# Weight tiles of 256 rows by 256 columns in a one-core attention and two-MoE kernel, with a new program order

## The chip, the cores and the metric

The kernel runs on one core of a Trainium2 chip. Its engines are TensorE (PE, with its weight loads as PEld), VectorE (DVE), ScalarE (ACT), GpSimd (POOL) and SyncE (SP), which issues nearly all DMAs. The metric is the device time of one execution in microseconds (us). Before the change it is 809.87 us, the median of three runs (809.11 to 810.15).

## The reference

Windowed attention with 32 global tokens per head, then a max-MoE of three matrices, then a gated MoE. All arrays are float32 in the reference; the weights reach the device as float64, as pairs of 32-bit words.

```
# q_l, k_l, v_l: (4, 8, 512, 64); q_g, k_g, v_g: (4, 8, 32, 64); window 32
out_g = softmax(q_g @ [k_g, k_l]^T / 8) @ [v_g, v_l]
out_l = softmax([q_l @ k_g^T / 8, masked(q_l @ k_l^T / 8)]) @ [v_g, v_l]
x = concat(out_g, out_l) as (2176, 512)
h = max(max(x @ w1, x @ w2), x @ w3)        # w1, w2, w3: (512, 768)
x = h @ w_out                               # w_out: (768, 512)
out = (sigmoid(x @ w_gate) * (x @ w_val)) @ w_out2
```

## The kernel before

**Stages.** From 0 to about 400 us attention and the first MoE run interleaved; from there to the end the second MoE runs, with dense matmuls. Tokens come in eight chunks `c` (four batches, two halves of 256 tokens each, the second with the 32 global tokens). A unit `t` is a pair of heads of a chunk. For the first two chunks PE transposes q and k (`tq`, `tk`, L532), DVE and ACT copy them out (`qw` L553, `kw` L557), PE makes scores (`sp`, L619), DVE masks them and takes the row minimum (`sm`, L625), ACT takes the exponential (L661), DVE multiplies by the reciprocal sum (`sm`, L675), PE transposes the result (`tp`, L683), ACT and DVE copy the two halves out (`pw`, L686 and L688), and PE multiplies with v (`ot`, L770). The result is scaled by ACT (`xw`, L790) and is the input of the first MoE.

**Weights of the first MoE.** `conv_a(i)` loads one raw tile of 512 KB (L302 for w1, w2, w3; L305 for `w_out`), 24 in all, 18 of them of the first three matrices. Tile `(wi, f)` holds all 512 rows (4 blocks of 128, `KD` = 4) of 128 columns, so a row of it is 1 KB in DRAM. Four steps turn float64 words into float32 (L287 on DVE or L285 on ACT, L289 on ACT, L291 and L294 on DVE), then ACT rounds a high part (L312) and POOL subtracts to get the low part (L271). The tile is then `ww[wi, f]` (whole float32) and `wa[wi, f]` (high and low).

**Layer 1.** `moe1_l1(c, f, wi, hold)` makes 128 output columns `f` of matrix `wi` for chunk `c`: four accumulating matmuls into a PSUM tile `ps` for chunk 0 (L882, whole float32), twelve for the other chunks (L321 to L323, three products of high and low parts). ACT copies the first of the three matrices out (`h`, L890), DVE takes the maximum with the second and third (L896, L893). The PSUM pool of `ps` has three buffers, which `tq` and `tk` share. Layer 2 (`moe1_l2`, L918 and L321 to L323) needs all six `f`.

**Order.** Every step is an entry of the list `ev`. The table `ORDER`, 3388 numbers, fixes in which order the entries are emitted, and with it the order of every engine and of the DMA queue; each engine runs its instructions strictly in that order. `SLOT` gives each raw and converted tile its place in SBUF.

Of the kernel before, what the change touches and what calls it, by code (L numbers as in the profile page):

```python
# [17 lines left out]
P = 128  # L18
# [185 lines left out]
def kernel(  # L204
# [92 lines left out]
    def conv_a(i):  # L297
# [8 lines left out]
        yield  # L306
        yield from to_f32(raw, i in LOW_ACT_A)
        hi = f32(raw[:, :, 1])
        ww[wi, f] = hi.rearrange("p (k f) -> p k f", k=KD) if cols else hi
        yield  # L310
        t = slot(("w", i), (2, DM), F32R)
        nc.scalar.copy(t[:, 0], hi)  # L312
# [1164 lines left out]
```

## Time and profile before

| what | us |
|---|---|
| median of three runs | 809.87 |
| the profiled execution, its own time | 809.25 |
| span of the profiled execution, first to last instruction | 807.5 |
| PE busy in it | 789.1 |
| DVE busy | 605.0 |
| ACT busy | 466.8 |
| POOL busy | 146.2 |

The profile is of one execution; 1.75 us of its time lie outside its span. PE is the busiest engine, so what counts is where PE is idle, and which engine or transfer ends each of these waits. Times in rows are us from the start of the span.

### The profile page before, as it was taken

Reading aid. Unit: us, or ns where it says so; the run is one execution under the profiler, and the core shown is the slowest. Engines: PE = TensorE matmul, PEld = TensorE weight load, DVE = VectorE, ACT = ScalarE, POOL = GpSimd, SP = SyncE. Lnnn points to the kernel's source line nnn. Section 1 sums busy time; section 2 is a strip of 40 time slices with the busy share of each in tenths; the row PEclk is TensorE's granted clock in tenths of the full one; section 3 lists DMA queues with packets and bytes.
Section 4 is the critical chain, followed back from the end, with each engine's and each line's share of the span. In section 5 each row is a group of like instructions: output and inputs, shape, how many; then the busy total and the mean of one; then the engine's idle time right before and its main releaser. Section 6 shows DMA issues by size and latency. Waiting matters only on the chain.

```text
span 807.5 us, 18056 instructions
## 1 busy us (share of the span) xinstructions
PE 789.1 (98%) x6854; PEld 751.9 (93%) x6854; DVE 605.0 (75%) x1303; ACT 466.8 (58%) x1119; POOL 146.2 (18%) x149
## 2 busy tenths in 40 slices
PE   6899999999999999999999999999999999999998
PEld 4678899999999899999999999999999999999998
DVE  4999987857766686863876878877675869876963
ACT  6887665747455584562657666665545366544532
POOL 3232566343242423332120000000000000000000
PEclk9999999999999999999999999999999999999999
DMA  9986545545456466454335266757252379635311
GB/s 211 265 232 171 120 93 101 112 82 118 88 104 116 95 106 104 77 99 114 140 101 184 92 185 210 242 194 235 99 179 82 121 253 314 196 109 187 118 43 56
DMA packets 217591, 116.08 MB, mean 144 GB/s; under 512 B 161056, under 2 KB 204576, under 8 KB 217504
## 3 DMA queue, kind: packets, MB, share of 16 engines
q1 hardware_dynamic: 216960, 114.80, 53.4%
q8 instruction: 54, 0.88, 0.5%
q14 instruction: 33, 0.27, 0.1%
q10 hardware_dynamic: 544, 0.13, 0.1%
HBM read 74.91 MB, written 28.57 MB: 128 GB/s over the span
## 4 chain that ended last, share of the span: by engine, by line
PE 86%; DVE 4%; ACT 3%; DMA 2%; SPq 2%; issue 1%; POOL 1%; DVEq 0%; POOLq 0%; ACTq 0%
PE pa L1038 18%; PE ps L321 9%; PE pe L1038 9%; PE ps L323 9%; PE ps L322 9%; PE pa L1225 9%; PE pb L1038 4%; PE pe L1225 4%; PE ps L882 3%; PE sp L619 3%; PE pb L1225 2%; PE ot L780 2%; PE ps L918 1%; PE acc L1202 1%; DMA pt<-pc 1%
## 5 line engine op out<-in xcount | busy, mean ns | idle before, releaser
L1038 PE MATMUL pa<-m,m 128*128 128x384 f32 (+1 forms) x864 | 155.0, 326 | 0.0
L321 PE MATMUL ps<-xt,m 128*128 128x288 f32 (+1 forms) x504 | 148.0, 294 | 1.7 <-DVE h L896 1.3
L323 PE MATMUL ps<-xt,m 128*128 128x288 f32 (+1 forms) x504 | 146.8, 291 | 0.0
L322 PE MATMUL ps<-xt,m 128*128 128x288 f32 (+1 forms) x504 | 145.1, 288 | 0.0
L1038 PEld LDWEIGHTS pa<-m,m 128*128 128x128 f32 x864 | 144.5, 188 | 0.1
L1044 ACT COPY sn<-pa 128x384 f32<-128x384 f32 (+1 forms) x108 | 49.5, 462 | 90.3 <-PE pa L1038 85.7
L321 PEld LDWEIGHTS ps<-xt,m 128*128 128x128 f32 x504 | 94.7, 188 | 6.9 <-issue 2.6
L322 PEld LDWEIGHTS ps<-xt,m 128*128 128x128 f32 x504 | 94.7, 188 | 0.1
L323 PEld LDWEIGHTS ps<-xt,m 128*128 128x128 f32 x504 | 94.6, 188 | 0.0
L1038 PE MATMUL pe<-m,m 128*128 128x384 f32 (+1 forms) x432 | 82.1, 327 | 0.0
L1038 PEld LDWEIGHTS pe<-m,m 128*128 128x128 f32 x432 | 72.6, 188 | 0.2 <-DVE sgt L1057 0.2
L1225 PE MATMUL pa<-m,m 128*128 128x256 f32 x576 | 72.2, 283 | 0.0
L1225 PEld LDWEIGHTS pa<-m,m 128*128 128x128 f32 x576 | 70.5, 192 | 0.1
L896 DVE TENSOR_TENSOR h<-ps,h 128x288 f32<-128x288 f32 (+1 forms) x90 | 39.1, 436 | 38.8 <-PE ps L323 30.0
L661 ACT ACTIVATE sm<-sm,st 128x224 f32<-128x224 f32 x128 | 60.9, 480 | 12.2 <-DVE st L625 12.1
L271 POOL TENSOR_TENSOR h<-h,h 128x288 fp32r<-128x288 f32 (+1 forms) x42 | 39.0, 932 | 105.3 <-ACT h L901 95.0
L707 DVE TENSOR_TENSOR pc<-sm,pc 64x512 f16<-64x512 f32 (+1 forms) x72 | 54.1, 751 | 3.6 <-ACT pc L704 1.7
L625 DVE CUSTOM_DVE_ANT_0 sm<-sp,mask 128x224 f32<-128x224 f32 x128 | 45.4, 381 | 6.7 <-PE sp L619 6.1
L1163 ACT CAST m<-m 128x768 fp32r<-128x768 f32 x44 | 35.8, 836 | 24.5 <-PE pa L1225 7.5
L1168 DVE TENSOR_TENSOR m<-m,m 128x768 fp32r<-128x768 f32 x44 | 41.1, 955 | 11.6 <-ACT m L1163 10.7
L321 PE MATMUL ps<-h,m 128*128 128x288 f32 (+1 forms) x168 | 49.2, 293 | 0.0
L322 PE MATMUL ps<-h,m 128*128 128x288 f32 (+1 forms) x168 | 48.6, 289 | 0.6 <-POOL h L271 0.6
(194 smaller groups left out, 1624.2 us busy)
## 6 DMA issues: line engine op xcount, KB each, us to landing
m<-in_moe_w_dram SPq DMA_DIRECT2D x18, 512.0 KB, 5.1
gd<-sgt SPq DMA_DIRECT2D x48, 192.0 KB, 3.6
m<-gd SPq DMA_DIRECT2D x6, 1536.0 KB, 7.8
m<-in_moe_w_val_dram SPq DMA_DIRECT2D x6, 1024.0 KB, 5.4
wr<-in_moe_w_out_dram SPq DMA_DIRECT2D x6, 1024.0 KB, 6.2
m<-in_moe_w_gate_dram SPq DMA_DIRECT2D x5, 1024.0 KB, 5.6
vr<-in_v_l_dram SPq DMA_DIRECT2D x48, 96.0 KB, 2.6
x2d<-x2s SPq DMA_DIRECT2D x32, 128.0 KB, 2.0
```

Of the source, the lines that this page charges most:

```text
L271: nc.gpsimd.tensor_tensor(out=out, in0=a, in1=f32(b), op=ALU.subtract)
L321: nc.tensor.matmul(ps, lhsT=wh, rhs=xh, start=first, stop=False)
L322: nc.tensor.matmul(ps, lhsT=wh, rhs=xl, start=False, stop=False)
L323: nc.tensor.matmul(ps, lhsT=wl, rhs=xh, start=False, stop=last)
L625: nc.vector.tensor_tensor_reduce(out=sm[:, hh, j], in0=sp[hh][:, j, 0:224], in1=mask[:, half + j, :], scale=-SC, scalar=3.0e38, op0=ALU.ad ...
L661: nc.scalar.activation(sm4[:, i], sm4[:, i], AF.Exp, bias=st[:, 0, i:i + 1], scale=-1.0, accum_out=st[:, 2, i:i + 1])
L707: nc.vector.tensor_tensor(out=l_, in0=s_, in1=h_, op=ALU.subtract)
L896: nc.vector.tensor_tensor(out=a, in0=ps[:, 0:n], in1=a, op=ALU.max)
L1038: nc.tensor.matmul(ps, lhsT=w[l][:, a, i], rhs=x[m][:, i], start=(k in (1, 2, 5) and i + l + m == 0), stop=(k in (2, 3, 4) and i == 1 and ...
L1044: nc.scalar.copy(t[:, 0:n], pend[u]["a"][:, 0:n])
L1168: tt(out=lo, in0=src[op], in1=f32(hi), op=ALU.subtract)
L1225: nc.tensor.matmul(ps, lhsT=g[l][:, f], rhs=wo_op(b, f, m), start=(k in (1, 2, 5) and f + l + m == 0), stop=(k in (2, 3, 4) and f == 5 and ...
```

## The change

`conv_a` loads, for w1, w2 and w3, tiles of 256 rows by 256 columns instead of 512 rows by 128 columns: tile `(wi, f)` is now column pair `f // 2` and row half `f % 2`. It is 512 KB as before, but a row of it is 2 KB in DRAM. `moe1_l1` takes its four row blocks from two tiles, `(wi, f - f % 2)` for the first two and the next one for the last two, and picks its 128 columns in them. `w_out`, the conversion steps, the number and size of matmuls and the `SLOT` table stay as they are. `ORDER` is another permutation of the same 3388 entries.

```
 ORDER = [
-    0, 57, 56, 62, 63, 64, 67, 68, 69, 256, 58, 74, 70, 75, 76, 59, 71, 153, 154, 77, 155, 78, 87, 1854, 161, 162, 79,
...
     def conv_a(i):
         f, wi = divmod(i, 3) if i < 3 * NF1 else (i - 3 * NF1, 3)
+        fp, kh = divmod(f, 2)
         src, cols = (w1, w2, w3, w_out)[wi], wi < 3
         raw = slot(("raw", i), (DM, 2), I32)
         if cols:
-            nc.sync.dma_start(out=raw.rearrange("p (k f) t -> p k (f t)", k=KD),
-                              in_=src[:, f * 2 * P:(f + 1) * 2 * P].rearrange("(k p) f -> p k f", p=P))
+            nc.sync.dma_start(out=raw.rearrange("p (k f) t -> p k (f t)", k=2),
+                              in_=src[kh * 2 * P:(kh + 1) * 2 * P, fp * 4 * P:(fp + 1) * 4 * P].rearrange("(k p) f -> p k f", p=P))
...
-        ww[wi, f] = hi.rearrange("p (k f) -> p k f", k=KD) if cols else hi
+        ww[wi, f] = hi.rearrange("p (k f) -> p k f", k=2) if cols else hi
...
-        wa[wi, f] = t.rearrange("p l (k f) -> p l k f", k=KD) if cols else t
+        wa[wi, f] = t.rearrange("p l (k f) -> p l k f", k=2) if cols else t
...
         ps = ps_mm.tile([P, CH], F32, tag="mm", name="ps1")
+        cols = slice(P * (f % 2), P * (f % 2) + P)
+        tiles = [(wi, f - f % 2 + k // 2) for k in range(KD)]
         if c in WHOLE1:
             for k in range(KD):
-                nc.tensor.matmul(ps[:, 0:n], lhsT=ww[wi, f][:, k], rhs=xt[c, k][:, 0, 0:n], start=(k == 0), stop=(k == KD - 1))
+                nc.tensor.matmul(ps[:, 0:n], lhsT=ww[tiles[k]][:, k % 2, cols], rhs=xt[c, k][:, 0, 0:n], start=(k == 0), stop=(k == KD - 1))
         for k in range(KD) if c not in WHOLE1 else ():
-            wt = wa[wi, f]
+            wt = wa[tiles[k]]
             x = xt[c, k]
-            mm3(ps[:, 0:n], (wt[:, 0, k], wt[:, 1, k]), (x[:, 0, 0:n], x[:, 1, 0:n]), k == 0, k == KD - 1)
+            mm3(ps[:, 0:n], (wt[:, 0, k % 2, cols], wt[:, 1, k % 2, cols]), (x[:, 0, 0:n], x[:, 1, 0:n]), k == 0, k == KD - 1)
```

Three places of the new order are shown. Line numbers of the changed kernel are one higher than before up to `moe1_l1`, and three higher in it and behind it. The first is the head of SP's DMA queue: `m_134` and `m_96` are q, `m_138` and `m_89` the last k rows with the global k, `m_137` and `m_88` the other k rows of chunk 0, each before and now.

```order
L432 DMA m_134<-in_q_l_dram 128x2x64 x2
L442 DMA m_138<-in_k_l_dram 32x8x64
L443 DMA m_138<-in_k_g_dram 32x8x64
L440 DMA m_137<-in_k_l_dram 128x6x64 x2
L432 DMA m_134<-in_q_l_dram 128x6x64 x2
L302 DMA m_180<-in_moe_w_dram 128x4x256
L385 DMA qgr<-in_q_g_dram 32x4x32 x4
```

```order
L443 DMA m_89<-in_k_l_dram 32x8x64
L444 DMA m_89<-in_k_g_dram 32x8x64
L433 DMA m_96<-in_q_l_dram 128x2x64 x2
L433 DMA m_96<-in_q_l_dram 128x6x64 x2
L441 DMA m_88<-in_k_l_dram 128x6x64 x2
L303 DMA m_186<-in_moe_w_dram 128x2x512
L303 DMA m_196<-in_moe_w_dram 128x2x512
L386 DMA qgr<-in_q_g_dram 32x4x32 x4
```

The last k rows now go ahead of the first q, and a weight tile has 512 words in a row instead of 256. The second place is PE around the first groups of layer 1, chunk 0.

```order
L683 MATMUL tp<-ident,sm 128x128 x8
L770 MATMUL ot<-pw,m_404 64x128 x16
L645 MATMUL sg<-kw,qgz_82 64x256 x2
L647 MATMUL sg<-kw,qgz_82 64x32 x2
L619 MATMUL sp<-kw,qw 128x224 x4
L645 MATMUL sg<-kw,qgz_82 64x256 x2
L882 MATMUL ps_568<-xw,m_376 128x256 x4
L882 MATMUL ps_581<-xw,m_235 128x256 x4
L882 MATMUL ps_588<-xw,m_180 128x256 x4
L683 MATMUL tp<-ident,sm 128x128 x8
```

```order
L684 MATMUL tp<-ident,sm 128x128 x8
L620 MATMUL sp<-kw,qw 128x224 x4
L646 MATMUL sg<-kw,qgz_82 64x256 x2
L648 MATMUL sg<-kw,qgz_82 64x32 x2
L646 MATMUL sg<-kw,qgz_82 64x256 x2
L771 MATMUL ot<-pw,m_425 64x128 x16
L885 MATMUL ps_569<-xw,m_241 128x256 x2
L885 MATMUL ps_569<-xw,m_374 128x256 x2
L684 MATMUL tp<-ident,sm 128x128 x4
L885 MATMUL ps_585<-xw,m_359 128x256 x2
L885 MATMUL ps_585<-xw,m_196 128x256 x2
```

The scores `sp` and `sg` moved from behind the products `ot` to ahead of them, and a group of layer 1 now reads two weight tiles. The third place is DVE a little earlier, between two multiplications L675 (L676 now).

```order
L667 RECIPROCAL st_238<-st_238 128x4
L675 TENSOR_TENSOR sm_237<-sm_237,st_238 128x896
L688 COPY pw_380<-tp_343 128x512
L287 TENSOR_SCALAR m12_376<-m12_376 128x512
L667 RECIPROCAL st_350<-st_350 128x4
L675 TENSOR_TENSOR sm_349<-sm_349,st_350 128x896
```

```order
L668 RECIPROCAL st_228<-st_228 128x4
L689 COPY pw_367<-tp_361 128x512
L676 TENSOR_TENSOR sm_227<-sm_227,st_228 128x896
L287 TENSOR_SCALAR m12_359<-m12_359 128x512
L287 TENSOR_SCALAR m14_374<-m14_374 128x512
L668 RECIPROCAL st_372<-st_372 128x4
L676 TENSOR_TENSOR sm_371<-sm_371,st_372 128x896
```

The copy `pw` of one half of the transposed scores now stands ahead of the multiplication for the next pair of heads.

## Rows read from the trace of the kernel before

**Rows 1.** The page: busy us, share of the span, instructions of the engines
```profile
PE 789.1 (98%) x6854; PEld 751.9 (93%) x6854; DVE 605.0 (75%) x1303; ACT 466.8 (58%) x1119; POOL 146.2 (18%) x149
```
**Rows 2.** Busy time by stretch: length, busy us per engine, clock, DMA share, GB/s
```profile
0.00:15.60 15.60, 9.70 (x38) 6.26 (x39) 5.59 (x23) 7.64 (x27) 6.36 (x26) 1.00 0.91 217
15.60:38.00 22.40, 17.60 (x164) 12.58 (x162) 21.88 (x56) 20.19 (x67) 4.44 (x4) 1.00 0.97 259
38.00:60.00 22.00, 20.19 (x108) 17.02 (x107) 20.39 (x55) 17.14 (x45) 8.65 (x6) 1.00 0.86 222
60.00:100.00 40.00, 39.80 (x277) 32.99 (x275) 39.79 (x93) 29.19 (x79) 14.57 (x11) 1.00 0.60 149
100.00:400.00 300.00, 297.61 (x3535) 280.79 (x3535) 215.94 (x607) 175.61 (x519) 108.05 (x99) 1.00 0.52 101
400.00:800.00 400.00, 400.00 (x2711) 398.26 (x2710) 299.37 (x472) 215.98 (x386) 4.15 (x4) 1.00 0.50 163
800.00:807.50 7.50, 4.22 (x36) 4.02 (x34) 2.08 (x4) 1.07 (x2) 0.00 (x0) 1.00 0.22 72
```
**Rows 3.** PE's waits: releaser, us in total, times, longest us
```profile
PE tq L532 <- DMA m<-in_q_l_dram: 4.5, 3, 3.1
PE tp L683 <- DVE sm L675: 1.8, 2, 1.4
...
PE tq L532 <- ACT h L890: 1.3, 1, 1.3
PE ps L321 <- DVE h L896: 1.3, 2, 1.0
...
PE ps L882 <- ACT kw L557: 0.5, 1, 0.5
```
**Rows 4.** PE's timeline: start, us, instruction, [idle before, releaser]
```profile
4.33 0.64 PE L532 MATMUL tk<-ident,m 128*128 128x128 f32 x2
5.42 0.34 PE L532 MATMUL tk<-ident,m 64*128 64x64 f32 x1 [0.46 <-DMA m<-in_k_g_dram]
...
19.90 0.33 PE L532 MATMUL tq<-ident,m 128*128 128x128 f32 x1 [0.87 <-DMA m<-in_q_l_dram]
...
27.06 1.09 PE L683 MATMUL tp<-ident,sm 128*128 128x128 f32 x8 [1.44 <-DVE sm L675]
...
34.00 1.86 PE L770 MATMUL ot<-pw,m 96*64 96x128 f32 x29 [1.13 <-DVE pw L688]
...
36.43 1.03 PE L619 MATMUL sp<-kw,qw 64*128 64x224 f32 x8
37.38 0.65 PE L645 MATMUL sg<-kw,qgz 128*64 128x256 f32 x4
37.97 5.46 PE L882 MATMUL ps<-xw,m 128*128 128x256 f32 x24
```
**Rows 5.** DMA totals of 24.95 to 27.85 (nearly all 1 KB packets)
```profile
DMA packets 1050, 1.05 MB, mean 362 GB/s; under 512 B 32, under 2 KB 1049, under 8 KB 1049
```
**Rows 6.** The same of 430 to 431.95 (nearly all 2 KB packets, of w_gate)
```profile
DMA packets 388, 0.79 MB, mean 403 GB/s; under 512 B 6, under 2 KB 6, under 8 KB 388
```
**Rows 7.** DVE's timeline between 16 and 34 us (columns as in rows 4)
```profile
16.78 0.42 DVE L287 TENSOR_SCALAR m<-m 128x512 int32<-128x512 uint32 x1
17.21 0.39 DVE L625 CUSTOM_DVE_ANT_0 sm<-sp,mask 128x224 f32<-128x224 f32 x1
...
17.84 0.69 DVE L294 SCALAR_TENSOR_TENSOR m<-m 128x512 int32<-128x512 int32 x1
...
22.75 1.47 DVE L294 SCALAR_TENSOR_TENSOR m<-m 128x512 int32<-128x512 int32 x1
...
28.06 1.09 DVE L675 TENSOR_TENSOR sm<-sm,st 128x896 f32<-128x896 f32 x1
...
33.25 0.70 DVE L688 COPY pw<-tp 128x512 f32<-128x512 f32 x1
```
**Rows 8.** POOL's timeline between 20 and 25 us
```profile
22.20 1.47 POOL L271 TENSOR_TENSOR m<-m,m 128x512 fp32r<-128x512 f32 x1 [14.62 <-ACT m L312]
```

337 rows, old and new, of the table ORDER are left out of this document.

## The prediction

> **What bounds the kernel now.** I read the page's totals first: PE is busy 789.1 us of a span of 807.5 [rows 1]. The change keeps every matmul, so only the remaining 18.4 us in which PE is idle can be won, plus whatever new waits it makes. Next, busy time by stretch [rows 2]: subtract PE's busy time from each length. PE idles 5.9 us up to 15.6, 4.8 from there to 38, 1.8 from 38 to 60, 0.2 from 60 to 100, 2.4 from 100 to 400, nothing from 400 to 800 and 3.3 in the last 7.5. The granted clock is 1.00, the upper level of 2.4 GHz, in every stretch, so no term below is a clock term. The DMA column is 0.91 and 0.97 in the first two stretches: loading is a limit there and nowhere else. DVE is busy 21.88 of 22.40 us in the second stretch and 39.79 of 40.00 from 60 to 100: there DVE is as full as PE. The list of PE's waits [rows 3] then says who ends them: q transfers (4.5 us in three waits, 3.1 of them the unavoidable first), DVE's multiply L675 (1.8), ACT's copy `h` (1.3) and DVE's maximum L896 (1.3 in two waits, behind 60). The question is which of some 12 us of waits before 60 go, and whether the time so won lasts until 400, where DVE-bound stretches can take it back.
>
> **The change part by part.**
>
> *Larger rows in DRAM.* Eighteen loads of 512 KB change from 1 KB rows to 2 KB rows. In 24.95 to 27.85, with nearly only 1 KB packets, the queue moved 362 GB/s [rows 5]; in 430 to 431.95, with nearly only 2 KB packets, 403 GB/s [rows 6]. 524288 bytes take 1.45 us at the first rate and 1.30 at the second: 0.15 us saved per tile. Where the queue is full, everything behind a tile lands that much earlier. Three tiles stand in the queue ahead of the q transfer that ends the wait of 0.87 at 19.90 [rows 4]: 3 x 0.15 = 0.45 us. PE's work up to that point is the same in both orders, so I take −0.45 there. The bounds are 0, if the transpose is then held by its input's successors instead (the copy `qw` comes next), and −0.87, the whole wait.
>
> The Trainium skill (DMA: Bandwidth & Descriptors, section "Where 436 GB/s comes from") says that loads from HBM into SBUF are bound on the HBM side, at about 358 GB/s. By it a tile would take an estimated 1.46 us in either shape and this term would be nothing. The trace shows 403 GB/s in a load of 2 KB rows [rows 6], above that figure, so here the measurement decides. That rule's outcome is a rival below.
>
> *Head of the queue.* The six first transfers are the same bytes in another order: the last k rows first, then q, then the rest of k. The sixth still lands at about 5.3 us. Before, what was left for PE at that time was one transpose of 64 columns, 0.34 us at 5.42; now the transposes that wait for the last of them take 0.64 us, as the two at 4.33 do [rows 4]. The first scores may begin some 0.3 to 0.6 us later. This ends in the wait for q at 19.90 (0.87 us, a DMA's), of which 0.42 are left after the term above, so it is absorbed: 0 taken, 0.6 − 0.42 = +0.2 as a bound.
>
> *From 19.90 to the first group of layer 1* (PE's row 96 in both orders, at 37.97 before [rows 4]). Two waits lie here that the order touches. At 34.00 PE waited 1.13 us for DVE's copy `pw` before the products `ot`. In the new order the scores `sp` and `sg` stand ahead of them, work that lies between 35.86, the end of the products, and 37.97 before: 2.1 us of cover for a wait of 1.13. It goes, unless `pw` is more than a microsecond later. At 27.06 PE waited 1.44 us for the multiply L675. In DVE's order the copy `pw` now goes ahead of the multiply. That gives the products their operand earlier by one multiply (1.09 us at 28.06) and makes the next transpose wait for a copy of 0.70 more [rows 7], but PE has work of that stretch to put in between. DVE itself is full, so I count its work up to the copy that stood at 33.25: one L287 fewer (−0.42), one L625 (+0.39) and one step L291 more (+0.69, as its twin L294 at 17.84): +0.66 us. Against this one two-input step fewer coincides with POOL: at 22.20 POOL's subtraction ran 1.47 us, and DVE's L294 at 22.75 took 1.47 instead of 0.69 [rows 7, 8], so one collision costs 0.78. The two cancel within 0.12. What is left is the 1.13 us wait, and of the 1.44 one the net of the swap, 1.09 − 0.70 = 0.39: −1.52 taken. The bounds are −2.57, both waits whole, and 0, if `pw` slips by as much as it was moved. Layer 1 then starts at 37.97 − 0.45 − 1.52 = 36.0.
>
> *A copy `xw` behind the last product.* The products now end right at the first group. Its third and fourth matmuls need the last two `xw`. A group is four matmuls in 1.82 us (5.46 for three groups [rows 4]), so two of them cover 0.9 us, and a copy of 128 x 256 can be bounded by the 0.70 us that one twice its size took on DVE [rows 7]. Nothing taken; +0.5 if ACT is late.
>
> *From 38 to 60.* Layer 1 of chunk 0 now takes two tiles per group but gets two groups from them, so its first three groups need six tiles instead of three. In DVE's order the last step of the sixth tile stands seven instructions behind the last copy `pw`, some 5 us of work; the third group begins 36.0 + 2 x 1.82 + 1.0 (transposes `tp`) = 40.6, and by that count the tile is ready at 39 to 40. The transpose `tq` then waited 1.3 us for a PSUM buffer, held by ACT's `h`, which stood behind the conversions [rows 3]. Now eight transposes `tp` stand between the three groups, so `tq` comes 1 us later relative to the first group while `h` can leave from the end of the first: the wait goes. The 0.5 us wait of layer 1 for `kw` [rows 3] goes in the same way. Against these 1.8 us I set 0.8 for a new wait of the groups for converted tiles, as DVE is at 20.39 of 22.00 us there [rows 2]. Taken: −1.0; bounds −1.8 and +1.0.
>
> *From 60 to 400.* PE arrives 3.0 us earlier (0.45 + 1.52 + 1.0) where DVE was full for 40 us [rows 2]. Its work there is the same, so what PE gained beyond DVE's own lead is given back in waits for L625, L675 or L896. DVE's lead is the conversion work that PE no longer waits for; I give back 0.9 us, the size of one of the waits for L896 (1.3 us in two, the longest 1.0 [rows 3]). Bounds: 0 and +5, which is seven chunks with about 0.7 each.
>
> *From 400 on.* PE has no idle time up to 800 [rows 2], the matmuls and the tail are the same: 0.
>
> **The sum.** −0.45 − 1.52 − 1.0 + 0.9 = −2.07 us. The profiled execution took 809.25 us (span 807.5, and 1.75 outside it, which stays), so this becomes 807.18. The median of the runs, 809.87, is 0.62 above the profiled one; with the same offset the forecast is 807.8.
>
> **The rivals.**
>
> *Six tiles instead of three (no change).* If DVE is later by the three extra conversions, the third group waits for them. A tile costs DVE an L291 and an L294, 2 x 0.69 = 1.4 us, and one more L287 of 0.42 where ACT doesn't do it [rows 7]. One and a half such tiles, 2.1 to 2.7 us, eat the gain between 20 and 60: with all of 1.52 + 1.0 = 2.5 us gone and 0.9 no longer there to give back, 809.87 − 0.45 = 809.4. For it speaks that DVE is busy 98% in 15.6 to 38 [rows 2]; against it that the counts up to the copy `pw` differ by under 0.1 us.
>
> *The PSUM pool in 100 to 400 (slower).* Layer 1 in later chunks uses three buffers `ps`, freed by `h` on ACT and by L896 on DVE. The new order interleaves other work there, and a wait for L896 cost up to 1.0 us, 1.3 in two [rows 3]. Without what is given back behind 60, the forecast would be 807.8 − 0.9 = 806.9. If each of the seven later chunks meets one more wait of 0.7 us on the average, the time is 806.9 + 4.9 = 811.8. It turns to slower, 811.5, from 4.6 us of such waits: five more than now at 1.0 each. Against it: DVE is busy 215.94 of 300 us there [rows 2], so it has room to catch up.
>
> *The shape brings nothing.* If the queue is bound elsewhere, as by the rule quoted above, the 0.45 us fall away: 808.25, the rest standing. For it speaks that the second stretch moved a mean of 259 GB/s at a DMA share of 0.97 [rows 2], so much of that time is not large packets.
>
> **How the numbers follow.** A change of 0.2% (1.6 us) is about what a measurement of this kernel can tell from none: below 808.25 is faster, above 811.5 slower. Chances: the forecast 0.56, six tiles 0.22, the PSUM pool 0.14, no gain from shape 0.08. The forecast lies only 0.45 us inside the bound of faster: so of its 0.56 some 0.08 are for times that land above it, within 0.2%, and 0.48 for faster; the last rival stands on the bound, 0.04 each way; the six-tile rival is within it, 0.22; the PSUM rival is slower, 0.14. Faster 0.52, same 0.34, slower 0.14. The range: the lower end takes the gain of 38 to 60 at its bound (0.8 more), nothing given back (0.9), the whole wait at 19.90 (0.42 more) and the rest of the 1.44 us wait (1.05): 807.8 − 3.2 = 804.6. The upper end takes in the six-tile rival and the pool rival up to 0.6 us per chunk (806.9 + 4.2 = 811.1), half of its chance: 811.1.
>
> **What would show it right or wrong.** Right: PE's first matmul of L885 (L882 before) starts near 36 us; the wait for q near 19.5 is under 0.5; no wait of `ot` for `pw` and none of `tq` for `h` in 38 to 60; a window with only weight tiles moves about 400 GB/s. Wrong: `ps` waits for DVE's L294 near 40 us (six tiles); a list of waits in 100 to 400 with five or more for the maximum, 4 us together (PSUM pool); still 362 GB/s in tile loads (shape). If PE is idle over 0.2 us anywhere from 400 to 800, the term of 0 there is wrong.

## The result and the profile after

The changed kernel takes 816.12 us, the median of six runs (814.46 to 819.62), against 810.01 for the kernel before; the ratio is 1.0082 (95% interval 1.0068 to 1.0096). It is slower by 6.6 us at the ratio, outside the range of the prediction and on its other side. The profiled execution took 819.62 us with a span of 817.2; it is the longest of the six, 3.5 us above their median, and the profiled execution before lies 0.8 below its own. So the two profiles are 10.4 us apart where the medians are 6.1 apart: up to 4.3 us of a difference read from them need not belong to the typical execution.

The page's totals and busy time by stretch, in the columns of [rows 1] and [rows 2]:

```profile
PE 792.9 (97%) x6854; PEld 753.6 (92%) x6854; DVE 611.5 (75%) x1303; ACT 465.9 (57%) x1119; POOL 150.3 (18%) x149
```

```profile
0.00:15.60 15.60, 10.24 (x43) 6.88 (x45) 6.06 (x25) 8.25 (x28) 6.39 (x26) 1.00 0.91 222
15.60:38.00 22.40, 19.07 (x164) 14.14 (x161) 20.68 (x54) 18.60 (x63) 2.59 (x2) 0.92 0.97 279
38.00:60.00 22.00, 20.55 (x120) 16.81 (x118) 21.86 (x52) 18.20 (x53) 9.69 (x7) 1.00 0.78 208
60.00:100.00 40.00, 35.86 (x240) 29.55 (x241) 39.38 (x87) 24.71 (x64) 11.02 (x9) 1.00 0.52 134
100.00:400.00 300.00, 293.78 (x3479) 275.01 (x3478) 210.71 (x606) 170.53 (x513) 115.00 (x100) 1.00 0.52 101
400.00:800.00 400.00, 399.55 (x2704) 397.48 (x2703) 306.77 (x475) 222.91 (x397) 5.64 (x6) 1.00 0.50 163
```

Up to 60 us PE idles 10.1 us (5.4, 3.3 and 1.5) where it idled 12.5 before: most of the 3.0 us that were forecast as a gain up to there. From 60 to 100 it idles 4.1 us instead of 0.2, with DVE as full as before, and from 100 to 400 it idles 6.2 instead of 2.4. PE's timeline shows the waits that went and those that came (columns as in [rows 4]):

```profile
19.20 0.30 PE L533 MATMUL tq<-ident,m 128*128 128x128 f32 x1 [0.87 <-DMA m<-in_q_l_dram]
...
29.06 1.06 PE L684 MATMUL tp<-ident,sm 128*128 128x128 f32 x8 [1.01 <-DVE sm L676]
...
37.14 2.00 PE L885 MATMUL ps<-xw,m 128*128 128x256 f32 x8
...
61.09 1.97 PE L885 MATMUL ps<-xw,m 128*128 128x256 f32 x8 [1.37 <-DVE m L294]
74.29 3.73 PE L885 MATMUL ps<-xw,m 128*128 128x256 f32 x16 [0.67 <-DVE m L294]
86.67 1.10 PE L771 MATMUL ot<-pw,m 96*64 96x128 f32 x16 [0.33 <-DVE stg L725]
91.14 1.11 PE L921 MATMUL ps<-hw,m 128*128 128x256 f32 x4 [0.57 <-ACT m L289]
92.79 0.71 PE L921 MATMUL ps<-hw,m 128*128 128x256 f32 x2 [0.55 <-DVE m L294]
94.42 8.48 PE L921 MATMUL ps<-hw,m 128*128 128x256 f32 x38 [0.92 <-DVE h L899]
```

The waits for `pw` at 34.0 and for ACT's `h` at 45.6 are gone ([rows 3, 4] before), though PE now waits 0.43 us for DVE's copy `pw` at 26.95, in front of an earlier product. Layer 1 and layer 2 of chunk 0 now wait for DVE's and ACT's conversion steps (L294, L289) and for DVE's `h`. The ends of layer 2 of chunk 0 and of PE's work are compared next. Before, they were these two rows:

```profile
99.42 0.60 PE L918 MATMUL ps<-hw,m 128*128 128x256 f32 x2
801.90 2.32 PE L1225 MATMUL pe<-m,m 128*128 128x256 f32 x18
```

In the changed kernel the first is the row from 94.42 above, and the second is

```profile
811.58 2.32 PE L1228 MATMUL pe<-m,m 128*128 128x256 f32 x18
```

Three points divide the loss of the profiled execution: the first group of layer 1 starts at 37.14 (37.97 before), the last matmul of layer 2 of chunk 0 ends at 102.9 (100.0 before), PE's last matmul ends at 813.9 (804.2 before). So −0.8 us up to layer 1, +3.7 from there to the end of chunk 0, and +6.8 behind it, +9.7 in all. (Five transposes `tpg` of the global scores, some 0.6 us, stood ahead of that end before and stand behind it now, so the two parts are rather 4.3 and 6.2.)

Behind 103 us, the list of waits (103 to 420) has this, all of it in waits of 0.8 us or less:

```profile
PE ps L322 <- ACT h L893: 2.1, 4, 0.8
PE ps L322 <- DVE h L899: 1.4, 3, 0.7
PE og L850 <- issue: 0.8, 1, 0.8
PE ps L323 <- DVE xt L799: 0.7, 1, 0.7
```

The first two rows are PE's waits for a PSUM buffer, 3.5 us in seven. They are not all new. The kernel before had three such waits behind 60 us, 1.7 us together:

```profile
PE ps L321 <- DVE h L896: 1.3, 2, 1.0
PE ps L321 <- ACT h L890: 0.4, 1, 0.4
```

One thing in this execution is not a cause: the granted clock was 0.53 and 0.62 of full speed in 20 to 22 and 22 to 24, so the lower level of 1.2 GHz for most of it, after PE had been busy 0.71 us of the stretch 18 to 20. The lower level is also in the profiled executions of the runs e2 and e3 below (0.92 as the mean of 15.6 to 38 in each), which were not slower than the kernel before. And two of the six executions of the changed kernel, of 814.46 and 815.62 us, show a mean granted clock of 1.00 over the whole span.

### The profile page after: what moved, and what is told of

The parts are those of the page before. It is cut to its first block, busy times and chain, and to the rows that moved or that the text cites. A ratio compares the mean times of both kernels' runs of the same rounds, so it can differ in the third digit from the quotient of the medians.

```text
span 817.2 us, 18048 instructions
## 1 busy us (share of the span) xinstructions
PE 792.9 (97%) x6854; PEld 753.6 (92%) x6854; DVE 611.5 (75%) x1303; ACT 465.9 (57%) x1119; POOL 150.3 (18%) x149
## 4 chain that ended last, share of the span: by engine, by line
PE 70%; DVE 9%; SPq 8%; DMA 6%; ACT 3%; issue 3%; POOL 2%; DVEq 0%; ACTq 0%; POOLq 0%
PE pa L1041 17%; PE pe L1041 9%; PE pa L1228 8%; PE ps L322 6%; PE ps L324 6%; PE ps L323 6%; PE pb L1041 4%; PE pe L1228 4%; PE pb L1228 2%; DMA m<-in_moe_w_dram 2%; SPq L514 2%; SPq L515 1%; DVE m L291 1%; DMA qr<-in_q_l_dram 1%; DVE sm L626 1%
## 5 line engine op out<-in xcount | busy, mean ns | idle before, releaser
L626 DVE CUSTOM_DVE_ANT_0 sm<-sp,mask 128x224 f32<-128x224 f32 x128 | 44.7, 381 | 10.1 <-PE sp L620 9.9
L271 POOL TENSOR_TENSOR h<-h,h 128x288 fp32r<-128x288 f32 (+1 forms) x42 | 39.3, 942 | 66.5 <-ACT h L904 43.2
```

The costliest lines, as they stand in the source:

```text
L271: nc.gpsimd.tensor_tensor(out=out, in0=a, in1=f32(b), op=ALU.subtract)
L626: nc.vector.tensor_tensor_reduce(out=sm[:, hh, j], in0=sp[hh][:, j, 0:224], in1=mask[:, half + j, :], scale=-SC, scalar=3.0e38, op0=ALU.ad ...
```

## What prolongs DVE

DVE's rows from 38 and 58 us, and POOL's at the same times:

```profile
38.63 2.98 DVE L287 TENSOR_SCALAR m<-m 128x512 int32<-128x512 uint32 x2
...
56.90 1.61 DVE L734 TENSOR_SCALAR eg<-eg,stg 128x640 f32<-128x640 f32 x1
58.43 1.79 DVE L291 SCALAR_TENSOR_TENSOR m<-m 128x512 int32<-128x512 int32 x1
60.26 0.69 DVE L294 SCALAR_TENSOR_TENSOR m<-m 128x512 int32<-128x512 int32 x1
60.87 0.69 DVE L291 SCALAR_TENSOR_TENSOR m<-m 128x512 int32<-128x512 int32 x1
```

```profile
38.28 3.05 POOL L271 TENSOR_TENSOR m<-m,m 128x512 fp32r<-128x512 f32 x2 [10.31 <-DMA m<-in_moe_w_dram]
```

```profile
55.59 4.08 POOL L271 TENSOR_TENSOR m<-m,m 128x512 fp32r<-128x512 f32 x3
```

An L291 takes 1.79 us at 58.43 and 0.69 at 60.87; two L287 take 2.98, where one took 0.42 in [rows 7]. Each of these long ones begins while a subtraction L271 runs on POOL and ends 0.3 to 0.6 us behind it: POOL's pair from 38.28 ends at 41.33 and DVE's at 41.61, POOL's three from 55.59 at 59.67 and the L291 at 60.22. I added up, for each kernel, what DVE's instructions took beyond the usual time of their form up to the end of the last conversion step (the 24th L294), and DVE's idle time. Prolonged instructions are called collisions below; "the rest" is DVE's busy time without what they were prolonged by.

| kernel | last L294 ends | prolonged by | instructions | DVE idle | the rest |
|---|---|---|---|---|---|
| before | 93.1 | 6.5 | 8 | 12.3 | 74.3 |
| changed | 96.4 | 11.3 | 11 | 12.0 | 73.1 |
| e1, new order, old tiles | 96.2 | 11.8 | 12 | 11.5 | 72.9 |
| e3, before without L271 on weights | 92.9 | 1.7 | 2 | 17.0 | 74.2 |
| e4, changed without it | 86.9 | 1.5 | 2 | 12.4 | 73.1 |
| e8, changed, L271 later | 96.0 | 9.9 | 10 | 12.5 | 73.6 |
| e9, changed, earlier releases | 95.3 | 11.2 | 11 | 10.9 | 73.2 |

All eight and eleven prolonged instructions of the two kernels overlap an instruction of POOL: seven and eight of them begin while an L271 runs, the others while another instruction of POOL does. DVE's own work is the same within 1.4 us. In the new order DVE's idle time is about the same with L271 and without it (12.0 us, and 12.4 in e4), so the 9.5 us by which its conversions end earlier in e4 are no shorter wait for transfers or other engines. Up to 38 us the new order does have fewer collisions (1.0 us instead of 4.0; up to 34, where the prediction counted, one instead of two); from 38 to 96 it has 10.4 us of them instead of 2.5. By the Trainium skill (SBUF — State Buffer, section "Who interferes with whom") a DVE instruction with two inputs in SBUF contends with a GpSimd instruction that reads SBUF, and so does a `tensor_scalar` in a two-port mode with any; whoever issues first holds the shared pair of ports for its whole instruction, and the other is blocked. The rows agree: the long ones begin while L271 runs, and end behind it by most of their usual time.

## The experiments

**Order or shape?** Two runs take the change apart.

e1 is the kernel before with the new `ORDER` and nothing else.

> The new order with the old tiles of 512 rows by 128 columns (1 KB rows in DRAM); the result is the reference's. If the order makes the loss, the time stays near the changed kernel's 816.1, between 815 and 818 (each of 18 tiles lands 0.15 us later). If the shape makes it (two tiles per group, larger packets), the loss goes: 809 to 811.5.

815.91 us, ratio 1.0072 (1.0049 to 1.0095). The loss comes with the order alone.

e2 is the other half, with the old order and the old use of the tiles:

```diff
-            nc.sync.dma_start(out=raw.rearrange("p (k f) t -> p k (f t)", k=KD),
-                              in_=src[:, f * 2 * P:(f + 1) * 2 * P].rearrange("(k p) f -> p k f", p=P))
+            nc.sync.dma_start(out=raw.rearrange("p (k f) t -> p k (f t)", k=2),
+                              in_=src[f % 2 * 2 * P:(f % 2 + 1) * 2 * P, f // 2 * 4 * P:(f // 2 + 1) * 4 * P].rearrange("(k p) f -> p k f", p=P))
```

> The old order and the old use of the tiles, but each raw tile of the first three matrices is loaded as 256 rows by 256 columns, so a row in DRAM is 2 KB; the products then take other weights than the reference. If long rows only shorten transfers, 809.0 to 810.2 (0 to 0.9 us gained at the waits for q). If long rows harm by themselves, above 813.

809.46 us, ratio 0.9999 (0.9980 to 1.0019), inside its first expectation: the shape shows no gain and no harm in the time. The interval is 1.5 us wide to either side, so a gain of 0.45 us is not excluded. The transfers themselves are faster, as expected: in the changed kernel, 32 to 36 us moved

```profile
DMA packets 814, 1.57 MB, mean 392 GB/s; under 512 B 48, under 2 KB 48, under 8 KB 814
```

against 362 GB/s in [rows 5].

**Collisions.** e3 and e4 leave out POOL's subtraction for weights in the old and in the new kernel; the product that used the low part takes the high part again (in layer 1 as shown for e3, and in layer 2 likewise):

```diff
-        sub(t[:, 1], hi, t[:, 0])
...
-            mm3(ps[:, 0:n], (wt[:, 0, k], wt[:, 1, k]), (x[:, 0, 0:n], x[:, 1, 0:n]), k == 0, k == KD - 1)
+            mm3(ps[:, 0:n], (wt[:, 0, k], wt[:, 0, k]), (x[:, 0, 0:n], x[:, 1, 0:n]), k == 0, k == KD - 1)
```

> The kernel before without GpSimd's subtraction for the low part of the first MoE's weights; the third product takes the high part a second time. Collisions with GpSimd cost DVE 6.5 us up to its last conversion step at 93 us, but PE waited only 0.2 us between 60 and 100. Theory collisions: 808.5 to 810 (PE had cover). Rival (GpSimd's steps stand in PE's path themselves): under 807.

> The changed kernel without the same subtraction. Collisions with GpSimd cost DVE 11.3 us up to its last conversion step at 96 us, and PE waited 4.1 us between 60 and 100 for conversions. Theory collisions: PE's waits from 60 to 100 fall under 1 us and the time by 3 to 4 us, to 812 to 813.5. Rival (the order lacks DVE time there whether GpSimd works or not): waits from 60 to 100 stay over 3 us and the time within 1 us of 816.

e3: 807.31 us, 0.9968 (0.9950 to 0.9985), a little under the expectation. e4: 805.34 us, 0.9946 (0.9930 to 0.9961), 10.8 us under the changed kernel and not the 3 to 4 that I expected. Without the collisions the new order is 2.0 us faster than the old one without them (807.31 − 805.34). That the prediction's sum gave the same size is luck: in the profiles it is 6.5 us won up to the end of chunk 0 (93.3 against 99.8) less 5.7 lost behind it (708.0 against 702.3), and neither is a term of that sum. Busy time of e4 from 38 to 100:

```profile
38.00:60.00 22.00, 22.00 (x138) 18.56 (x137) 20.90 (x60) 19.86 (x57) 0.00 (x0) 1.00 0.67 186
60.00:100.00 40.00, 39.81 (x303) 34.03 (x302) 35.73 (x86) 27.17 (x71) 5.26 (x5) 1.00 0.62 157
```

PE idles 0.2 us in these 62 instead of 5.6, and layer 2 of chunk 0 ends at 93.3 instead of 102.9:

```profile
83.61 9.74 PE L921 MATMUL ps<-hw,m 128*128 128x256 f32 x44 [0.18 <-issue]
```

Why I expected too little: I counted PE's waits from 60 to 100 as all that there was to win. But DVE was behind from 38 us on, and PE's waits showed only what was left of that after PE's own work had covered the rest; with DVE in time, PE could also have gone faster than the old order does. In the old order the same removal moves the end of layer 2 only from 100.0 to 99.8: DVE's time won there goes into idle time (17.0 instead of 12.3 us in the table), because PE sets the pace. In the new order DVE sets it, so nearly every prolonged instruction counts.

e8 moves each of the 24 subtractions as late in POOL's queue as the slots allow, and nothing else.

> The changed kernel, but each of GpSimd's 24 subtractions for weights is issued as late as the slots of its tile allow; nothing else moves and the result is the reference's. If collisions with GpSimd pace the stretch to 103 us, the end of layer 2 of chunk 0 moves by as much as DVE's sum of prolonged instructions up to its last conversion (11.3 us before): 1 us less there, 1 us earlier. Rival (DVE's work paces it, wherever GpSimd works): end at 102 to 103 whatever that sum becomes, 815 to 817.

Collisions fell by 1.4 us only, and the end of layer 2 from 102.9 to 102.4. That is the direction of the theory, but too small a step to tell it from the rival. The time is 822.56 us, 1.0161 (1.0135 to 1.0186), outside both expectations, for a reason that I had not thought of: chunk 1 then waits for the low parts.

```profile
PE ps L324 <- POOL m L271: 6.7, 2, 3.6
```

So the subtractions can't simply be put off.

**Where in the order?** Three spliced orders, all with the old tiles.

> Old tiles; the order is the new one up to the first group of layer 1 (224 entries), and then the old one. If the head of the new order is a gain and the rest of it the loss: layer 1 starts near 36 us, the lead of 1.5 to 2 us lasts as DVE has cover in the old rest, 807.8 to 809. Rival (what PE wins at the head is given back between 60 and 100): 809.5 to 810.5.

> Old tiles; the new order up to the first group of layer 1 of chunk 1 (594 entries), and then the old one. If the loss has two places, collisions before 103 us and PSUM waits behind: the last matmul of layer 2 of chunk 0 ends at 102.6 as in the run with new order and old tiles, the rest takes 704 to 705 us as in the kernel before, together 812 to 813.5. Rival (all the loss comes from arriving late at 103, which disturbs the rest): 815.5 or more. Rival (all of it comes from the later order): under 811.

> Old tiles; the old order up to the first group of layer 1 (228 entries), and then the new one. If the loss lies behind 38 us: layer 1 starts at 38, layer 2 of chunk 0 ends at 102.5 to 104, 815 to 818. Rival (the new head starves DVE of conversions, and so makes the waits from 60 on): 810 to 812.

e5: 810.54 us, 1.0028 (1.0011 to 1.0045), at the upper edge of its second expectation. e6: 815.44, 1.0088 (1.0066 to 1.0109). e7: 824.99, 1.0205 (1.0177 to 1.0233), outside both. They settle less than I hoped, since each seam makes waits of its own that are in neither order; the largest, of e7 (first row) and e5:

```profile
53.30 0.98 PE L532 MATMUL tk<-ident,m 128*128 128x128 f32 x3 [8.37 <-DVE h L896]
```

```profile
44.40 0.44 PE L532 MATMUL tq<-ident,m 128*128 128x128 f32 x2 [2.70 <-ACT h L890]
52.61 1.06 PE L683 MATMUL tp<-ident,sm 128*128 128x128 f32 x8 [2.64 <-ACT pw L686]
```

What can be used: in e5 layer 1 starts at 35.4 us, 2.6 earlier than before, so the head of the new order does bring a gain; behind it stand the two seam waits of 5.3 us, more than that. e6 came out at its second expectation (815.5), but 3.5 us of seam waits at 112 and 134 us are in it, so the verdict stays open there.

**The waits behind 103 us.** In e1 and in the changed kernel groups of layers 1 and 2 wait, five of them at the same places in the order, for a PSUM buffer that is still held, because its release stands behind two or three other instructions of ACT or DVE. They don't come from the late end of chunk 0: in e4, where it ends 9.6 us earlier, 4.1 us of such waits are left.

```profile
PE ps L322 <- DVE h L899: 2.7, 2, 2.4
PE ps L322 <- ACT h L893: 1.4, 3, 0.6
```

ACT's rows of the changed kernel around the wait of PE that ended at 255.6:

```profile
253.64 1.66 ACT L705 CAST pc<-sm 64x512 f16<-64x512 f32 x3
255.21 0.36 ACT L893 COPY h<-ps 128x256 f32<-128x256 f32 x1
```

```profile
255.62 0.40 PE L322 MATMUL ps<-h,m 128*128 128x288 f32 x1 [0.76 <-ACT h L893]
```

Three casts stand ahead of the copy `h`, and PE's next group waits for the buffer that it frees. e9 moves nine such releases ahead, four in ACT's queue and five in DVE's, in numbers of `ORDER` alone. One of them, in ACT's queue:

```diff
-L705 CAST pc<-sm 64x512 x2
-L705 CAST pc<-sm 128x8x32
-L893 COPY h_3147<-ps_3118 128x288
+L705 CAST pc<-sm 64x512
+L893 COPY h_3128<-ps_3110 128x288
+L705 CAST pc<-sm 64x512
+L705 CAST pc<-sm 128x8x32
```

> The changed kernel, with nine steps of layer 1 in chunks 1 to 5 that release a PSUM buffer (the copy L893 or the maximum L899) moved two or three instructions ahead in the queue of their own engine; six of them ended PE waits of 3.3 us together in the changed kernel. If the releases stood too far back in a queue: those waits shrink to under 1 us and the time to 812.5 to 814. Rival (the buffers are short because layer 1 itself arrives in bursts, and the waits move to other groups): 815.5 to 817.

814.01 us, ratio 1.0041 (1.0030 to 1.0052), where the changed kernel had 1.0082: half of the loss by the ratios, 2.1 us by the medians. The waits from 103 to 420 us:

```profile
PE ps L323 <- DVE xt L799: 0.5, 1, 0.5
PE og L850 <- DMA ptg<-pcg: 0.5, 1, 0.5
PE ps L322 <- ACT h L893: 0.5, 2, 0.3
```

The waits for releases fell from 3.5 to 0.5 us, and the stretch from the end of chunk 0's layer 2 to PE's last matmul from 711.0 to 705.4 us (704.2 before). Of these 5.6 us the waits explain 3.0; the profiled execution of e9 is 1.6 us under its median and that of the changed kernel 3.5 above, so the rest may be the two executions. The first expectation holds, its time at the upper edge: the place in the queue set these waits, and they did not move elsewhere. As the old order had 1.7 us of them too, e9 took away more than the 1.8 us that the new order had added.

**Both at once.** e13 puts e9 and e4 together; e14 is e9 with `nc.vector.tensor_tensor` in place of `sub`.

> The changed kernel with both suspected causes taken away together: the nine releases moved ahead as before, and no GpSimd subtraction for weights (the third product takes the high part again). If collisions and release places are separate and are all of the loss, the parts add: layer 2 of chunk 0 ends near 93, the rest takes 704 to 706 us, 801 to 803.5, which is 4 to 6 us under the old order without the subtraction (807.3). Rival (they are one loss seen twice): 804.5 to 806.

> The changed kernel with the nine releases moved ahead, and the 24 subtractions for weights on DVE instead of GpSimd; the result is the reference's. If a collision costs DVE as much as it prolongs an instruction (0.8 us a piece, 9.8 us for 13 of them), the subtraction done by DVE itself costs 13 x 0.7 = 9.1 us in the same stretch: layer 2 of chunk 0 ends at 101 to 102 and the time is 812.5 to 815. Rival (the trace overstates what a collision costs): DVE's path grows by more than 3 us, 816 or more.

e13: 806.06 us, 0.9942 (0.9915 to 0.9968), just above the rival's range and no better than e4. In its trace the rest behind chunk 0 took 703.7 us, a little less than expected (708.0 in e4), but layer 2 ended at 96.7 and not 93.3, for which I have no reason; its five runs lie between 801.7 and 806.9. So the releases save time behind chunk 0 with the collisions gone too, but that the two causes add in the time is not shown, and the rival is not excluded. e14: 818.55 us, 1.0112 (1.0092 to 1.0132). Layer 2 of chunk 0 ended at 100.5 us (101.7 in e9, 96.7 in e13), a little earlier than expected. That agrees with a collision costing DVE about what the trace shows: 13 subtractions of its own, 0.69 us each, are no dearer. Behind that, the other eleven delay it, and the waits of chunk 1 came back:

```profile
PE ps L322 <- DVE h L899: 2.0, 1, 2.0
PE ps L324 <- DVE m L315: 1.2, 1, 1.2
```

The time lies where the rival put it, but not for the rival's reason; the expectation had left these waits out.

**Single moves in the old order.** e10 takes one move of the new order alone, on PE (and in ACT's queue the copy `xw` of the moved product):

```diff
-L770 MATMUL ot<-pw,m_404 64x128 x16
 L645 MATMUL sg<-kw,qgz_82 64x256 x2
 L647 MATMUL sg<-kw,qgz_82 64x32 x2
 L619 MATMUL sp<-kw,qw 128x224 x4
 L645 MATMUL sg<-kw,qgz_82 64x256 x2
+L770 MATMUL ot<-pw,m_404 64x128 x16
```

> The kernel before with one move of the new order alone: the scores of pair 5 and the global scores of pairs 2 and 5 ahead of the products of pair 2 (and the copy of the first product with them). If step c of the prediction holds: the wait of 1.13 us for the copy at 34.0 goes, layer 1 starts at 36.5 to 37, 808.5 to 809.2. Rival (the copy or DVE comes later by as much): 809.5 to 810.5.

e11 also moves ACT's copy of the first group ahead; e12 two releases in chunks 1 and 2 as well.

```diff
+L890 COPY h_599<-ps_568 128x256
 L312 CAST m_601<-m_450 128x512
 L289 ACTIVATE m_422<-m_422 128x512
-L890 COPY h_617<-ps_568 128x256
```

> As the run before, and in ACT's queue the copy h of the first group of layer 1 ahead of two conversion steps. The 1.3 us wait of the transposes at 45.6 goes: 807 to 808.3. Rival (layer 1 then waits for the weight conversions that ACT does later): 808.5 to 810.

> As the run before, and the releases of two groups of layer 1 in chunks 1 and 2 (waits of 1.0 and 0.4 us at 127.6 and 176.1) three and two instructions ahead in their queues. 806 to 807.5 if queue places set these waits; as the run before if they don't.

e10: 808.72 us, 0.9978 (0.9966 to 0.9990). e11: 809.05, 0.9979 (0.9967 to 0.9992). e12: 807.32, 0.9972 (0.9957 to 0.9988). All three are faster than the kernel before, by 0.2 to 0.3%, and so than the changed one. e10 and e12 are within their expectations, e11 is in its rival's range. e10's rows:

```profile
37.80 1.10 PE L770 MATMUL ot<-pw,m 96*64 96x128 f32 x16 [0.48 <-ACT xw L790]
38.83 5.46 PE L882 MATMUL ps<-xw,m 128*128 128x256 f32 x24
44.12 1.04 PE L683 MATMUL tp<-ident,sm 128*128 128x128 f32 x8
45.03 0.44 PE L532 MATMUL tq<-ident,m 128*128 128x128 f32 x2
```

The wait for `pw` is gone and one of 0.48 us for an `xw` has come. Layer 1 starts no earlier in this execution (38.83), but `tq` does not wait for `h` any more, so that the step that e11 adds had little left to win. The intervals of e10, e11 and e12 overlap: what the second and third step add is not settled.

## Why the prediction was wrong

- **Long rows, −0.45:** the transfers are faster (392 GB/s against 362). The wait at 19.90 ended at 19.20, still 0.87 us long; in the time e2 shows nothing. The rival that the shape brings nothing is not told apart from a gain of 0.45 us by the time; the limit that it rested on, one rate for either shape, did not hold.
- **From 19.90 to layer 1, start at 36.0:** right in the sum. In the profiled execution layer 1 starts at 37.14, with the lower clock from 20 to 24 in it; in e1, e5, e6, e8 and e9, which have the same head, at 35.4 to 36.1. The wait for `pw` at 34.0 went, the one for the multiply shrank from 1.44 to 1.01 us (0.39 were taken). What the prediction left out is a new wait for `pw` ahead of an earlier product, 0.43 us here and 2.42 in e9.
- **From 38 to 60, −1.0:** right in kind, too large. Both waits went, but PE's idle time there fell from 1.8 to 1.5 us only, as two new waits for DVE (0.58 and 0.60) stand in it.
- **From 60 to 400, +0.9 with bounds 0 and +5:** this is the step that failed. PE's idle time grew by 3.9 us from 60 to 100 and by 3.8 from 100 to 400, 7.8 together in the profiles, where 0.9 were taken. I had written that PE arrives earlier where DVE is full, and then priced what DVE takes back by the size of one wait for L896, instead of by DVE's own path. That path has three terms, and I looked at one. DVE's work was the same, as I said. Its collisions with POOL I had counted up to 34 us and taken as cancelled; behind 38 us they grew from 2.5 to 10.4, and the old trace had the price of one (0.78 [rows 7, 8]; 1.03 is the mean of eleven in the new trace). Without L271 on weights (e4) the end of chunk 0 moves from 102.9 to 93.3 and the time from 816.1 to 805.3. The third term is argued, not tested: a PE that is to be 6.7 us faster (93.3 against 100.0) needs conversions earlier by as much, so cover that the old order had is gone.
- **The rival of the PSUM pool** named a second part of the loss: 0.14 was too little for it. Its mechanism was right (buffers held until a release behind other work), its size too large: not 4.6 us and more of new waits but 1.8 (3.5 in seven, 1.7 before), of up to 0.8 us, and four of the seven on ACT's copy and not on DVE's maximum. I had argued against it with DVE's mean load of 72%. The mean says nothing about the place of one instruction in a queue that runs in order.
- **The rival of the six tiles** was not the cause: layer 1 waits for L294 at 61 and 74 us (2.0 us), and not for the sixth tile at 40. In e1, with one tile per group, these two waits are not there, yet others for DVE (0.81, 0.63 and 0.77 us) are, and chunk 0 ends at 102.6: DVE is late whichever tile is asked for.
- **From 400 on, 0:** PE is idle 0.45 us from 400 to 800, over the 0.2 that was named as the sign of a wrong term, but small beside the loss.

Left unexplained: of the 6.8 us behind 103 us in the profiled execution, 4.3 are idle time, of which 1.8 are releases; for the other waits (0.4 to 0.8 us each, for DVE's `xt`, `st` and `kt` and for the products `og`) no run was made. In 2.5 us PE is busy longer without a wait that the profile shows; some 0.6 of it are the five transposes, and as the two profiles are 4.3 us further apart than the medians, the rest may be no part of the typical loss.

## What to carry to other kernels

A new order of all engines is not judged by the waits of the old trace that it removes: walk the engine that becomes the bound through its whole queue, with what shares a port with it beside it. A release of a PSUM buffer belongs in its engine's queue right where its group ends; two or three instructions ahead of it cost TensorE up to 0.8 us each time here, on engines that were busy 57% and 70% of the time from 100 to 400. And an order that was spliced at a seam is a third order: single moves (e9, e10) told more than halves.

## What the runs showed of the hardware

Which DVE instructions POOL prolongs was clearer than I had thought. Over both traces together, with and without an overlapping L271: L287 (`tensor_scalar`) takes 0.95 and 0.47 us on the mean, L675 (two inputs in SBUF) 1.33 and 1.09, L707 (two inputs, two shapes together) 1.08 and 0.64, L733 (`tensor_scalar`) 1.02 and 0.58, L601 (a copy of bf16) 0.75 and 0.37. Those that read PSUM (L625, L896, L688), and transposes within SBUF (L569), don't change: L625 0.38 and 0.38 (61 overlaps), L896 0.44 and 0.44 (31 overlaps), L688 0.68 and 0.68, L569 0.44 and 0.44. (Those without an overlap of L271 may overlap another POOL instruction, so the second means are bounds from above.)
